# The opening of a sliding-window attention and feed-forward kernel: mask by a prefix sum, unshifted V for the first chunks, and another order of loads, scores and transposes

## The chip, the cores and the metric

One core of a Trainium2 chip (trn2) runs the whole program. The metric is device time in microseconds; the kernel before was run three times and its median is 326.21 us. A trace of one execution shows what each engine did: PE is TensorE, PEld its weight loads, DVE is VectorE, ACT is ScalarE, POOL is GpSimd, SP is SyncE. In the timeline rows the columns are start and duration in us, then engine, line, operation, output<-inputs, and in brackets the idle time before the row with what ended it.

## The reference

Attention with a causal window of 64 positions over 8 batches, 8 heads, 576 positions and 64 dimensions per head, and a gated feed-forward block (SiLU) on its output. Inputs and output are float32.

```python
def _attn_ref(q, k, v):
    scores = np.matmul(q, k.transpose(0, 1, 3, 2)) / np.sqrt(D)
    rel = pos[:, None] - pos[None, :]
    mask = (rel >= 0) & (rel < 64)
    scores = np.where(mask, scores, -1000000000.0)
    ...  # softmax over the last axis
    return np.matmul(attn, v)

def _moe_ref(x, w_gate, w_val, w_out):      # x: (4608, 512)
    g = x @ w_gate                          # (512, 1536)
    return (g * (1.0 / (1.0 + np.exp(-g))) * (x @ w_val)) @ w_out
```

## The kernel before

The 8 x 576 = 4608 tokens are cut into 36 chunks of 128. A chunk n holds two blocks of 64 queries. Each block sees its own 64 keys and the 64 before them, so the scores of a chunk are two triangles for each block: the lower one on its own keys, the upper one on the previous keys. One tile of 128 key rows by 128 query columns per head (`pt`) holds both.

Every operation is put on one engine's list, in the order in which the program names it (`_Graph.op`), and semaphores are added where data passes between engines. Each engine works through its list strictly in that order. The loads of q, k, v and of the weights are issued from POOL (`load`, `load2`, `load_w`); only the very first k load is issued from SP and ACT. Each POOL issue has a semaphore lane of its own, 16 in turn.

The program has an opening whose order is written by hand (`loads` and the first part of `build`), and a long remainder whose order stands in the lists `EARLY`, `LOADS` and `SHIPS`. The remainder chooses PSUM banks with a planner; the opening takes them from the list given to `banks`.

The opening goes like this:

- `warm(count, n)` issues matmuls on a tile of zeros (`wz`) into a PSUM bank that nobody reads: fillers.
- `first_loads` and `first_cast` bring the first 256 tokens of k, half by SP and VectorE, half by ACT and ScalarE. `first_T` transposes them on TensorE, `first_ev` copies them out.
- `load2` brings the first 256 tokens of q (stage 0) and the next 256 of k and q (stage 1); `T2` transposes them (L426) and copies them out.
- `init_ident` makes the identity with an affine select on POOL. `init_mask` makes three variants of the 0/1 mask of a chunk: two affine selects on POOL, then three instructions on VectorE (L333 to L335). `init_nmask` turns them into 0 and -30000.
- `Sa(n, True)` writes that bias into two PSUM banks with two 512-wide identity matmuls (L459); `Sb` adds the scores of chunk n (L479, L483) and lets ScalarE take the exponential (L491). From chunk 4 on the scores get no bias, and the 0/1 mask is multiplied in afterwards (`Sm`).
- The product of `pt` with V comes in three forms. `AVs` (L612) multiplies over all 128 key rows at once; as the rows of the first query block are not in the order of V's rows, it needs a copy of V shifted by 64 rows (`vs`, made by `shift` on POOL or ScalarE out of `va`). `AVmm` (L580) uses 64 x 64 quadrants of the array and reads `va` of this and the previous chunk directly; it has two phases of 16 matmuls, and phase 1 has a semaphore wait for phase 0. Chunk 0 has no predecessor and uses one matmul per head (L609).
- `AVn` divides by the row sums on VectorE: a reciprocal (L628) and a multiplication (L631).
- `X` transposes a finished chunk (L743) into `xT`, and `Fs` does the feed-forward for some of the 12 columns of 128: a gate block and a value block of matmuls (L818), a tanh on ScalarE (L825), and two VectorE instructions (L827, L829). The output multiplication is L850.

The PSUM data of phase 0 and phase 1 are joined in the array's accumulation; the wait between them is this argument of the second call:

```python
done.append(self.g.op("pe", pe, reads=rd, writes=[b[1] for b in bx],
                      after=done[0] if phase else None))
```

The functions that the change touches, and what calls them, with the line numbers of the profile before:

Of the kernel before, what the change touches and what calls it, by code (L numbers as in the profile page):

```python
# [7 lines left out]
ALU = mybir.AluOpType  # L8
# [158 lines left out]
class _Kernel:  # L167
# [41 lines left out]
    def alloc(self):  # L209
# [93 lines left out]
    def init(self):  # L303
        g = self.g
        self.zero(self.wup[:, :], ["wup"])
        g.op("act", lambda e: e.activation(self.wup[:, :], self.wup[:, :], ACTF.Exp), writes=["wup"])
        self.zero(self.wz[:, :], ["wz"])
        self.zero(self.ident[:, :], ["ident"])
        self.zero(self.mask[:, :], ["mask"], 1.0)
        self.init_va(0, 4)  # L310
        for i in range(3):
            self.zero(self.vs[i][:, :, 64:80], [("vs", i, 0), ("vs", i, 1)], 1.0)
# [9 lines left out]
            pattern=[[-1, 128]], channel_multiplier=1), writes=["ident"])  # L322

    def init_mask(self):
        g = self.g
        mm = self.mask[:, :].rearrange("p (v e q) -> p v e q", v=3, e=2)
        a, b = mm[:, :, 0, :], mm[:, :, 1, :]
        for fill, base in ((0.0, 0), (1.0, 64)):
            g.op("pool", lambda e, fill=fill, base=base: e.affine_select(
                out=a, in_=a, compare_op=ALU.is_ge, fill=fill, base=base,  # L330
                pattern=[[0, 3], [1, 64]], channel_multiplier=-1), writes=["mask"])
        src = mm[:, 0:1, 0, :].to_broadcast([128, 3, 64])
        one = g.op("dve", lambda e: e.tensor_scalar(b, src, -1.0, 1.0, ALU.mult, ALU.add), reads=["mask"], writes=["mask"])  # L333
        g.op("dve", lambda e: e.memset(mm[64:128, 1, 0, :], 0.0), writes=["mask"])
        g.op("dve", lambda e: e.memset(mm[0:64, 2, 1, :], 0.0), writes=["mask"], after=one)  # L335

    def init_nmask(self):
        self.g.op("dve", lambda e: e.tensor_scalar(
            self.nmask[:, :], self.mask[:, :], 1.0, 30000.0, ALU.subtract, ALU.mult), reads=["mask"], writes=["nmask"])

    def init_kmask(self):
        g = self.g
# [558 lines left out]
    def loads(self):  # L901
        self.first_loads()
        self.load2(0, "q")
        self.load2(1, "k")
        self.init()
        self.init_ident()
        self.first_cast("k", 0, "dve")
        self.init_mask()
        self.load2(1, "q")
        self.load(0, "v")  # L910
        self.load(1, "v")
        self.load(2, "v")
        self.load(3, "v")
        self.load_w("g", 0, 2)
        self.load_w("v", 0, 2)
# [81 lines left out]
    def main(self, t):  # L997
# [109 lines left out]
    def build(self):  # L1107
        F, S, AV, X, T2, O = self.F, self.S, self.AV, self.X, self.T2, self.O
        self.loads()
        self.banks("a", [0, 1, 2, 3, 4, 5, 6, 7, 0, 1, 4, 5, 2, 3, 0, 1, 6, 7, 4, 5, 2, 3, 0, 1, 6, 7, 2, 3])  # L1110
        self.banks("f", [4, 5, 0, 1, 6, 7, 2, 3])
        self.warm(84, n=58)
        self.first_cast("k", 1, "act")
        self.init_nmask()
        k0 = self.first_T("k")
        self.first_ev("k", k0, 0, "dve")
        self.first_ev("k", k0, 1, "act")
# [26 lines left out]
        self.AVs(a2)  # L1144
        self.AVn(a2)
        a3 = self.AVa(3)
        self.AVs(a3)
# [12 lines left out]
        next(f2, None)  # L1160
        next(f1)
        next(f1, None)
        for n in range(4):
# [54 lines left out]
```

## Time and profile before

| | |
|---|---|
| median of 3 runs | 326.21 us (326.02 to 330.19) |
| profiled execution, its own time | 325.66 us |
| its span, first to last instruction | 323.9 us |
| TensorE busy | 315.4 us, 97% |
| VectorE / ScalarE / POOL busy | 204.1 / 136.1 / 109.8 us |
| granted TensorE clock, mean | 1.000 |

The span lies within the execution's time; what is around it is start and end of the program. A share of busy time is a mean over stages, so the opening has to be read from its own rows. The chain of waits follows the work that ended last back to what released it.

### The profile page before, as it was taken

The numbers are of one execution on the slowest core, as the hardware profiler recorded it, in microseconds if no ns is written. First come the engines' busy times: TensorE is split into PE (matmuls) and PEld (weight loads), VectorE is DVE, ScalarE is ACT, GpSimd is POOL, SyncE is SP. The second block draws the span as 40 slices with busy tenths as digits, with TensorE's granted clock in tenths as the row PEclk, the third lists the DMA queues.
The fourth block names the chain that finished last, engine by engine and source line by source line (L and its number), as shares of the span: only waits on it lengthen the run. The fifth ranks groups of instructions, "written<-read, shape, count | busy, mean of one in ns | idle before, by whom it ended". The sixth has DMA issues, their size and how long they took to land.

```text
span 323.9 us, 7964 instructions
## 1 busy us (share of the span) xinstructions
PE 315.4 (97%) x3395; PEld 170.3 (53%) x3430; DVE 204.1 (63%) x355; ACT 136.1 (42%) x244; POOL 109.8 (34%) x138
## 2 busy tenths in 40 slices
PE   8899999999999999999999999999999999999996
PEld 7585588855455444545454444545454544444443
DVE  5678888853657738666657575756666566555510
ACT  4735854545354335433334343525252522322322
POOL 8999990007930703315050607070502000000000
DMA  9999999999999996969699989999976202000012
GB/s 145 176 190 169 170 175 153 143 140 120 141 156 143 117 161 111 151 163 150 147 159 166 157 137 113 134 127 135 119 119 74 67 34 64 35 32 33 32 67 97
DMA packets 165412, 39.85 MB, mean 123 GB/s; under 512 B 152705, under 2 KB 160641, under 8 KB 165377
## 3 DMA queue, kind: packets, MB, share of 16 engines
q0 software_dynamic: 115152, 18.62, 82.1%
q1 hardware_dynamic: 44896, 11.22, 26.0%
q10 hardware_dynamic: 5328, 9.51, 8.1%
q8 instruction: 27, 0.44, 0.6%
q14 instruction: 9, 0.07, 0.1%
HBM read 37.75 MB, written 9.44 MB: 146 GB/s over the span
## 4 chain that ended last, share of the span: by engine, by line
PE 92%; ACT 2%; DMA 2%; issue 1%; POOL 1%; DVE 0%; POOLq 0%
PE ps L818 57%; PE ps L850 28%; PE ps L661 2%; DMA va<-in_v_dram 2%; ACT pt L491 1%; PE ps L883 1%; PE ps L516 1%; ACT pt L528 1%; PE ps L479 1%; PE ps L423 1%; PE ps L743 1%; POOL qs L381 0%; PE ps L483 0%; PE ps L612 0%; ACT vs L296 0%
## 5 line engine op out<-in xcount | busy, mean ns | idle before, releaser
L818 PE MATMUL ps<-xT,Wv 128*128 128x512 bf16 (+1 forms) x486 | 110.5, 351 | 0.5
L818 PE MATMUL ps<-xT,Wg 128*128 128x512 bf16 (+1 forms) x479 | 107.6, 351 | 2.4 <-issue 1.4
L827 DVE SCALAR_TENSOR_TENSOR uu<-sig,ps 128x512 bf16<-128x512 bf16 (+1 forms) x109 | 74.0, 679 | 56.4 <-ACT sig L825 55.7
L825 ACT ACTIVATE sig<-ps 128x512 bf16<-128x512 f32 (+1 forms) x109 | 64.9, 597 | 79.8 <-PE ps L818 78.7
L850 PE MATMUL ps<-Wo,hT 128*128 128x512 bf16 x413 | 94.7, 379 | 0.6 <-ACT pt L491 0.3
L829 DVE SCALAR_TENSOR_TENSOR hT<-uu,ps 128x512 bf16<-128x512 bf16 (+1 forms) x109 | 74.3, 682 | 3.7
L818 PEld LDWEIGHTS ps<-xT,Wv 128*128 128x128 bf16 x496 | 48.5, 98 | 44.9
L369 POOL DMA_DIRECT2D kn<-in_k_dram x31 | 29.3, 949 | 122.8 <-PE ps L850 93.5
L818 PEld LDWEIGHTS ps<-xT,Wg 128*128 128x128 bf16 x496 | 46.6, 98 | 41.4
L850 PEld LDWEIGHTS ps<-Wo,hT 128*128 128x128 bf16 x420 | 40.9, 98 | 48.7
L857 ACT ACTIVATE ost<-ps 128x512 f32<-128x512 f32 x35 | 20.9, 597 | 89.9 <-PE ps L850 83.9
L369 POOL DMA_DIRECT2D va<-in_v_dram x40 | 36.0, 955 | 12.3 <-PE ps L850 12.3
L369 POOL DMA_DIRECT2D qn<-in_q_dram x31 | 29.5, 960 | 0.0
L688 DVE RECIPROCAL rp<-ps 128x14 f32<-128x14 f32 (+1 forms) x28 | 5.7, 203 | 36.0 <-PE ps L661 36.0
L491 ACT ACTIVATE pt<-ps 128x512 bf16<-128x512 f32 x36 | 19.0, 597 | 4.4 <-PE ps L483 4.1
L690 DVE TENSOR_TENSOR xb<-ps,rp 128x896 bf16<-128x896 f32 (+1 forms) x28 | 19.4, 692 | 1.0
L528 ACT ACTIVATE pt<-ps 128x512 bf16<-128x512 f32 x36 | 18.6, 602 | 2.3 <-PE ps L520 2.1
L661 PEld LDWEIGHTS ps<-va,pt 64*64 64x64 bf16 x888 | 10.8, 107 | 6.1 <-issue 5.5
L661 PE MATMUL ps<-va,pt 64*64 64x65 bf16 x888 | 13.4, 194 | 0.1
L543 DVE TENSOR_TENSOR pt<-pt,kmask 128x1024 bf16<-128x1024 bf16 x18 | 12.3, 684 | 0.0
L543 DVE TENSOR_TENSOR pt<-pt,mask 128x1024 bf16<-128x1024 bf16 x13 | 8.7, 686 | 0.8 <-ACT pt L491 0.8
L893 DVE COPY ost<-ps 128x128 f32<-128x128 f32 x1 | 0.3, 291 | 11.8 <-PE ps L883 11.8
(72 smaller groups left out, 151.0 us busy)
## 6 DMA issues: line engine op xcount, KB each, us to landing
out_dram<-ost ACTq DMA_DIRECT2D x35, 256.0 KB, 2.1
va<-in_v_dram POOLq DMA_DIRECT2D x32, 128.0 KB, 6.2
kn<-in_k_dram POOLq DMA_DIRECT2D x25, 128.0 KB, 4.9
qn<-in_q_dram POOLq DMA_DIRECT2D x25, 128.0 KB, 5.4
Wg<-in_moe_w_gate_dram POOLq DMA_DIRECT2D x6, 256.0 KB, 7.4
Wv<-in_moe_w_val_dram POOLq DMA_DIRECT2D x6, 256.0 KB, 7.1
Wo<-in_moe_w_out_dram POOLq DMA_DIRECT2D x2, 768.0 KB, 18.2
qs<-in_q_dram POOLq DMA_DIRECT2D x3, 256.0 KB, 8.6
```

The source lines that it names most:

```text
L369: self.g.op("pool", lambda e, d=d, a=a: e.dma_start(d, a), writes=ks, dma=True, after=self.hold)
L491: g.op("act", lambda e, po=po, p=p: e.activation(po, sv[p], ACTF.Exp, scale=SCALE), reads=[bx[p][1]], writes=[pk[p]])
L528: g.op("act", lambda e, po=po, p=p: e.activation(po, sv[p], ACTF.Exp, scale=SCALE), reads=[bx[p][1]], writes=[pk[p]])
L543: self.g.op("dve", lambda e: e.tensor_tensor(pt, pt, m, ALU.mult), reads=pk + [key], writes=pk)
L661: z = e.matmul(self.psa[64 * c:64 * c + 64, o:o + 65], pt[p][rows, h, 64 * a:64 * a + 64], va[m][rows, h, 0:65], start=first, stop=phase = ...
L690: g.op("dve", lambda e, d=d, num=num, rb=rb: e.tensor_tensor(d, num, rb, ALU.mult), reads=bk + [("rp", k)], writes=xk, cost=(1.0, 0.25)[k])
L818: r = e.matmul(bank[:, a * n:a * n + n], W[:, kk, f * 128:f * 128 + 128], xT[:, kk, lo:hi], start=(kk == 0), stop=(kk == NK - 1))
L825: g.op("act", lambda e, G=bank: e.activation(sig[:, 0:w], G[:, 0:w], ACTF.Tanh, scale=0.5), reads=[bk], writes=[("sig", i)])
L827: g.op("dve", lambda e: e.scalar_tensor_tensor(uu[:, 0:w], sig[:, 0:w], 1.0, G[:, 0:w], ALU.add, ALU.mult), reads=[("sig", i), gk], writes ...
L829: g.op("dve", lambda e: e.scalar_tensor_tensor(out, v3(uu), 0.5, v3(V), ALU.mult, ALU.mult), reads=[("uu", i), vk], writes=[("hT", ih, f) ...
L850: r = e.matmul(OB[:, :], hT[:, f, 128 * u:128 * u + 128], self.Wo[:, f, :], start=(f == 0), stop=(f == NF - 1), skip_group_check=mid is no ...
L857: g.op("act", lambda e: e.activation(ost[:, :], OB[:, :], ACTF.Copy), reads=[ok], writes=[("ost", io)])
```

## The change

It concerns the opening alone.

- The mask is made on VectorE: the identity is extended by its own first 64 columns, and `tensor_tensor_scan` runs along the columns adding the identity and subtracting the identity moved by 64 columns, starting from 0 for the first 64 rows and from 1 for the others (`edge`). The two affine selects on POOL go. `nmask` is made out of this one variant, in two variants in place of three. The other two variants of the 0/1 mask are copied in a new function, `init_masks`, which runs at the step `V` of the remainder.
- On POOL the identity comes ahead of the second k load; the second q load, the four V loads and the weights follow without anything between them.
- Chunks 1 to 3 use `AVmm` in place of `AVs`, so their six shifted copies (four on POOL, two on ScalarE) go.
- 40 fillers of 121 columns stand in place of 84 of 58; three fillers ahead of the second k transpose go, two come ahead of the second q transpose.
- The bias of chunk 2 comes ahead of product 0. The transposes of chunks 2 and 3 stand between the gate block and the value block of the first feed-forward step, and the second half of tokens for columns 0 and 1 comes ahead of the columns 2 and 3.

```diff
-        self.ident = sb("ident", 128)
+        self.id3 = sb("ident", 192)
+        self.ident = self.id3[:, 0:128]
+        self.edge = sb("edge", 1, F32)
...
-        self.nmask = sb("nmask", 3 * 128)
+        self.nmask = sb("nmask", 2 * 128)
...
-        self.zero(self.mask[:, :], ["mask"], 1.0)
+        self.zero(self.edge[0:64, :], [("edge", 0)])
+        self.zero(self.edge[64:128, :], [("edge", 1)], 1.0)
...
     def init_mask(self):
+        g.op("dve", lambda e: e.tensor_copy(self.id3[:, 128:192], self.id3[:, 0:64]), reads=["ident"], writes=["id3"])
+        g.op("dve", lambda e: e.tensor_tensor_scan(
+            self.mask[:, 0:128], self.id3[:, 0:128], self.id3[:, 64:192], self.edge[:, 0:1], ALU.add, ALU.subtract),
+            reads=["ident", "id3", ("edge", 0), ("edge", 1)], writes=["mask"])
+
+    def init_masks(self):
+        two = self.mask[:, 0:128].unsqueeze(1).to_broadcast([128, 2, 128])
+        out = self.mask[:, 128:384].rearrange("p (v x) -> p v x", v=2)
+        one = self.g.op("dve", lambda e: e.tensor_copy(out, two), reads=["mask"], writes=["mask"])
...  # two memsets of a quarter each, as before
-        for fill, base in ((0.0, 0), (1.0, 64)):
-            g.op("pool", lambda e, fill=fill, base=base: e.affine_select(
...
     def loads(self):
         self.first_loads()
         self.load2(0, "q")
-        self.load2(1, "k")
         self.init()
         self.init_ident()
+        self.load2(1, "k")
+        self.load2(1, "q")
+        self.init_mask()
+        self.init_nmask()
         self.first_cast("k", 0, "dve")
-        self.init_mask()
-        self.load2(1, "q")
-        self.load(0, "v")
...
-        self.load_w("g", 2, 4)
-        self.shift(0, 1, "pool")
-        self.shift(1, 1, "pool")
-        self.load_w("v", 2, 4)
-        self.shift(2, 1, "pool")
-        self.shift(3, 0, "pool")
-        self.W(4, 6)
-        self.W(6, 8)
+        for n in range(4):
+            self.load(n, "v")
+        for f in range(0, 8, 2):
+            self.W(f, f + 2)
...
         elif w == "V":
             self.init_va(4, self.NV)
+            self.init_masks()
...
-        self.warm(84, n=58)
+        self.warm(40, n=121)
...
         self.Sb(s0)
-        self.warm(3, j=0)
         T2(1, "k", ("dve", "dve"))
         self.Sb(s1)
+        self.warm(2, j=4)
         T2(1, "q", ("dve", "act"))
         self.start()
+        s2 = self.Sa(2, True)
         a0 = self.AVa(0)
         self.AVs(a0)
-        self.shift(1, 0, "act")
         self.AVn(a0)
-        s2 = self.Sa(2, True)
         self.Sb(s2)
-        self.shift(2, 0, "act")
         a1 = self.AVa(1)
-        self.AVs(a1)
+        self.AVmm(a1, 0)
+        self.AVmm(a1, 1)
...  # chunks 2 and 3 in the same way
         f0 = self.Fs(0, (0, 1), 0, 256)
         next(f0)
-        next(f0)
         X(2, "act", "a")
         X(3, "dve", "a")
+        next(f0)
         next(f0, None)
-        f1 = self.Fs(0, (2, 3), 0, 256)
-        next(f1)
         f2 = self.Fs(0, (0, 1), 256, 512)
         next(f2)
         next(f2)
         next(f2, None)
+        f1 = self.Fs(0, (2, 3), 0, 256)
+        next(f1)
         next(f1)
         next(f1, None)
```

More of the change, by code (lines that the diff above doesn't have):

```diff
@@ L325, in init_mask @@
         g = self.g
-        mm = self.mask[:, :].rearrange("p (v e q) -> p v e q", v=3, e=2)
-        a, b = mm[:, :, 0, :], mm[:, :, 1, :]
-        for fill, base in ((0.0, 0), (1.0, 64)):
[L329 to L335, printed above, removed]
+        g.op("dve", lambda e: e.tensor_copy(self.id3[:, 128:192], self.id3[:, 0:64]), reads=["ident"], writes=["id3"])
[3 more added lines that the diff above has]
+    def init_masks(self):
+        mm = self.mask[:, :].rearrange("p (v e q) -> p v e q", v=3, e=2)
+        two = self.mask[:, 0:128].unsqueeze(1).to_broadcast([128, 2, 128])
+        out = self.mask[:, 128:384].rearrange("p (v x) -> p v x", v=2)
+        one = self.g.op("dve", lambda e: e.tensor_copy(out, two), reads=["mask"], writes=["mask"])
+        one = self.g.op("dve", lambda e: e.memset(mm[64:128, 1, 0, :], 0.0), writes=["mask"], after=one)
+        self.g.op("dve", lambda e: e.memset(mm[0:64, 2, 1, :], 0.0), writes=["mask"], after=one)
     def init_nmask(self):
-        self.g.op("dve", lambda e: e.tensor_scalar(
-            self.nmask[:, :], self.mask[:, :], 1.0, 30000.0, ALU.subtract, ALU.mult), reads=["mask"], writes=["nmask"])
+        two = self.mask[:, 0:128].unsqueeze(1).to_broadcast([128, 2, 128])
+        out = self.nmask[:, :].rearrange("p (v x) -> p v x", v=2)
+        one = self.g.op("dve", lambda e: e.tensor_scalar(out, two, 1.0, 30000.0, ALU.subtract, ALU.mult), reads=["mask"], writes=["nmask"])
+        self.g.op("dve", lambda e: e.memset(self.nmask[64:128, 128:192], -30000.0), writes=["nmask"], after=one)
     def init_kmask(self):
@@ L1143, in build @@
         a2 = self.AVa(2)
-        self.AVs(a2)
+        self.AVmm(a2, 0)
+        self.AVmm(a2, 1)
         self.AVn(a2)
         a3 = self.AVa(3)
-        self.AVs(a3)
+        self.AVmm(a3, 0)
+        self.AVmm(a3, 1)
         self.AVn(a3)
```

8 lines of the change are left out of this document (1 added, 7 removed).

## The prediction

> **What bounds the kernel now.** I read the page first, then busy time by stretch, the chain of waits over the first 18 us, the transfers of that stretch, and last the timeline row by row. The page and the stretches:
>
> ```profile
> span 323.9 us, 7964 instructions
> PE 315.4 (97%) x3395; PEld 170.3 (53%) x3430; DVE 204.1 (63%) x355; ACT 136.1 (42%) x244; POOL 109.8 (34%) x138
> 0.00:16.00 16.00, 13.52 (x306) 10.11 (x308) 9.40 (x29) 9.14 (x16) 13.94 (x24) 1.00 1.44 160
> 66.00:314.00 248.00, 244.92 (x2431) 118.79 (x2458) 152.27 (x251) 97.27 (x174) 63.09 (x75) 1.00 1.04 113
> ```
>
> TensorE is the bound, and past the opening it hardly pauses (244.92 of 248 us busy). After the opening every engine's order of work is the same in both kernels but for three small mask instructions on VectorE. So the result is a shift of the point at which TensorE goes over to the dense feed-forward matmuls (L818, at 15.92 us). The ceiling of any gain is what TensorE does not do in the first 16 us: 16.00 - 13.52 = 2.5 us, under 0.8% of the time, and 1.3 of it lie before its first instruction.
>
> What leads to that point is told by the chain of waits:
>
> ```profile
> 6.27 6.03 DMA va<-in_v_dram
> ...
> 12.32 0.63 ACT vs L296
> ...
> 14.44 1.06 ACT pt L491 x2
> ...
> 15.54 0.44 PE ps L612 x14
> ```
>
> The second V chunk lands at 12.30 (6.27 + 6.03), ScalarE makes its shifted copy, TensorE multiplies with it, and so on to the last attention product (L612 at 15.54). The timeline has the same chain, with what stands around it:
>
> ```profile
> 1.29 4.24 PE L789 MATMUL ps<-wz 128*128 128x58 bf16 x84 [1.29 <-DVE wz L301]
> 2.33 0.88 POOL L381 DMA_DIRECT2D ks<-in_k_dram  x1
> 3.29 0.32 POOL L320 TENSOR_SCALAR_AFFINE_SELECT ident<-ident 128x128 bf16<-128x128 bf16 x1
> 3.54 0.87 POOL L329 TENSOR_SCALAR_AFFINE_SELECT mask<-mask 128x192 bf16<-128x192 bf16 x2
> 4.09 0.60 DVE L298 CAST ost<-hT 128x512 bf16<-128x512 f32 x1 [1.39 <-DMA hT<-in_k_dram]
> 4.50 0.91 POOL L381 DMA_DIRECT2D qs<-in_q_dram  x1
> 4.69 0.63 ACT L296 ACTIVATE ost<-hT 128x512 bf16<-128x512 f32 x1 [1.69 <-DMA hT<-in_k_dram]
> 5.12 0.34 DVE L338 TENSOR_SCALAR nmask<-mask 128x384 bf16<-128x384 bf16 x1
> 5.38 0.78 PE L769 MATMUL ps<-ident,ost 128*128 128x128 bf16 x8
> 5.99 0.59 PE L459 MATMUL ps<-nmask,ident 128*128 128x512 bf16 x2
> 8.62 0.82 PE L789 MATMUL ps<-wz 128*128 128x512 bf16 x3
> 8.74 1.08 ACT L491 ACTIVATE pt<-ps 128x512 bf16<-128x512 f32 x2 [0.95 <-PE ps L483]
> 10.64 0.64 PE L426 MATMUL ps<-ident,qs 128*64 128x128 bf16 x16 [0.27 <-DMA qs<-in_q_dram]
> 11.39 0.60 ACT L296 ACTIVATE qT<-ps 128x512 bf16<-128x512 bf16 x1
> 11.59 0.40 PE L609 MATMUL ps<-va,pt 128*128 128x65 bf16 x8 [0.31 <-DMA va<-in_v_dram]
> 13.01 0.22 PE L612 MATMUL ps<-vs,pt 128*64 128x65 bf16 x1 [0.20 <-ACT vs L296]
> 13.38 0.60 PE L459 MATMUL ps<-nmask,ident 128*128 128x512 bf16 x2
> 13.92 0.24 PE L479 MATMUL ps<-qT,kT 64*64 64x128 bf16 x2
> 14.29 0.62 PE L743 MATMUL ps<-ident,xb 128*128 128x128 bf16 x8
> 14.40 1.08 ACT L491 ACTIVATE pt<-ps 128x512 bf16<-128x512 f32 x2
> 15.92 0.28 PE L818 MATMUL ps<-xT,Wg 128*128 128x256 bf16 x1
> ```
>
> Read from it: product 1 starts at 13.01; the bias matmuls of scores 3 follow at 13.38 (0.37 later), the scores at 13.92 (0.54), the next matmuls at 14.29 (0.37); the two exponentials end at 15.48, 1.56 after the scores began; product 3 starts 0.06 later, the feed-forward 0.38 after that.
>
> **The change, part by part.**
>
> *Mask.* The two affine selects (0.87 us) leave POOL; VectorE gets a 64-column copy, a scan over 128 columns, an nmask of 256 columns and a memset. No row shows a scan. Its bounds are nothing and 0.69, twice the 384-column nmask of L338; I take 0.34, the row of L338 itself, the nearest. The identity now goes ahead of the k transfer on POOL and is ready near 2.33 + 0.08 + 0.32 = 2.73, so VectorE runs to about 3.8 and is free for its cast at 4.09. Cover: the first transposes wait for ScalarE's cast (4.69 + 0.63 = 5.32), so VectorE may be 0.6 us late. TensorE reads nmask first at 5.99, when it has long been ready (5.12 + 0.34 = 5.46): an earlier mask brings nothing by itself. Cost 0, with the worst scan too.
>
> *Fillers.* 84 x 58 = 4872 columns against 40 x 121 = 4840: the same 4.2 us, and the transposes start with the cast in either case. Of the three 512-wide fillers at 8.62, two come back later, ahead of the second q transpose, which waits for its transfer anyway. Cost 0.
>
> *Loads.* The second k load is issued about 0.45 us later (2.33 to 2.8), the second q load some 0.85 earlier, the four V loads 0.9 earlier, the later weights up to 4 us earlier, as the shifted copies that stood between them are gone. That helps only if the transfers waited for their issue:
>
> ```profile
> GB/s 0 0 0 0 70 139 340 393 221 166 173 159 163 178 153 155 196 146 150 157 155 155 154 156 169 178 194 195 197 196 197 224 183 190 193 191 197 194 197 198
> ```
>
> These are 40 slices of 0.5 us. From 2.5 us on there is no hole: the transfers run at a level rate with work queued, and they keep their order. So q still lands at 10.6 and V at 11.5 and 12.3. I take 0; the bound is the 0.85 us by which the issue moves.
>
> *No shifted V for chunks 1 to 3.* Each product goes from 16 matmuls over 128 rows (L612) to two phases of 16 quadrant matmuls (L580), where phase 2 waits for phase 1. No row has this pair back to back with 16; the last attention pair has it with 32, and a phase of 16 stands elsewhere:
>
> ```profile
> 269.34 1.00 PE L661 MATMUL ps<-va,pt 64*64 64x65 bf16 x64
> 270.50 0.81 PE L818 MATMUL ps<-xT,Wg 128*128 128x512 bf16 x3 [0.16 <-issue]
> 269.33 0.36 PEld L661 LDWEIGHTS ps<-va,pt 64*64 64x64 bf16 x32 [0.42 <-issue]
> 269.87 0.36 PEld L661 LDWEIGHTS ps<-va,pt 64*64 64x64 bf16 x32 [0.17 <-PE ps L661]
> 33.90 0.32 PE L580 MATMUL ps<-va,pt 64*64 64x65 bf16 x16
> 34.38 0.81 PE L818 MATMUL ps<-xT,Wg 128*128 128x512 bf16 x3 [0.16 <-issue]
> ```
>
> With 32 each, the second phase starts 0.54 after the first and the whole takes 1.00, so a phase lasts 0.46 and the hand-over 0.08. With 16 a phase lasts 0.32: the pair takes 0.32 + 0.08 + 0.32 = 0.72, and 0.16 pass before a full-width matmul (both rows of L818): 0.88 until the next work, against 0.37 to 0.38 for L612 now. Bounds: 0.48, if one phase vanished beside the other (33.90 to 34.38), and 1.16, that of the 32 form (269.34 to 270.50). I take 0.88, as it is built from 16-matmul rows.
>
> [...]
>
> *The chain, added up.* Product 1 now waits for V itself: 12.30 + 0.06 = 12.36 in place of 13.01, that is -0.65. Scores 2 must be done by then: q lands at 10.6, its ScalarE copy ends at 11.99 at the latest, the scores start at 12.0 and take 0.37, so it just fits. Product 1 costs +0.51 (0.88 - 0.37); bias and scores 3 to the end of their exponentials stay at 0.54 + 1.56; product 2 lies under those exponentials; product 3 costs +0.50 (0.88 - 0.38). The feed-forward starts at 12.36 + 0.88 + 0.54 + 1.56 + 0.06 + 0.88 = 16.28, against 15.92: **+0.36 us**.
>
> *Transposes 2 and 3 between gate and value.* Now they stand behind two blocks, afterwards behind one:
>
> ```profile
> 16.47 0.69 DVE L631 TENSOR_TENSOR xb<-ps,rc 128x512 bf16<-128x512 f32 x1
> 17.67 0.61 PE L743 MATMUL ps<-ident,xb 128*128 128x128 bf16 x8
> 18.15 1.92 PE L818 MATMUL ps<-xT,Wg 128*128 128x256 bf16 x16
> 28.55 0.69 DVE L827 SCALAR_TENSOR_TENSOR uu<-sig,ps 128x512 bf16<-128x512 bf16 x1 [0.32 <-ACT sig L825]
> ```
>
> The cover shrinks by one block, (17.67 - 15.92) / 2 = 0.87 us. Now the last scaling ends at 17.16, 1.62 after product 3 began (15.54). Afterwards product 3 begins at 15.40 and is 0.28 longer (0.72 - 0.44): the scaling ends at 17.30. The gate block ends at 16.28 + 0.87 = 17.15, chunk 2's transposes take 0.24, chunk 3's start at 17.39. It fits by hundredths: 0, and up to 0.4 if VectorE is later. The half-blocks that change places put the later-loaded weight columns last, so no new wait there.
>
> *Mask, second part.* A copy and two memsets join VectorE's work near 25 us, by the row of L338 at most 3 x 0.34 = 1.0, likelier 0.5. VectorE waits 0.32 us for ScalarE by 28.55, slack that takes most of it up; uncovered it would cost 0.5. I take 0.
>
> **The sum.** The profiled execution took 325.66 us: its span of 323.9 and 1.76 around it. 325.66 + 0.36 = 326.0. The median of the runs shown, 326.21, is 0.55 above that execution, so against the median 326.5 to 326.6; I say 326.5, +0.1%.
>
> **The rivals.**
>
> *A. The loads do come earlier, or the phases are cheap.* For: q and V are issued some 0.85 sooner. Against: the level rate above. If q lands at 9.8, its copy still waits on ScalarE for the exponentials of scores 0 and 1 (8.74 + 2 x 1.08 = 10.9), ends at 11.5, scores 2 start near 11.6 and product 1 near 11.97: -0.39, and the sum is 0.0, or 326.2. If instead the pair takes 0.48, it is 0.36 - 0.80 = -0.44, or 325.8; both together -0.83, or 325.4.
>
> *B. TensorE idles behind the transposes.* Chunk 3's transposes stand behind one block in place of two. At 0.4 us late the time is 326.9. For: it fits by hundredths. Against: VectorE has nothing else queued then.
>
> *C. The clock is lost.* With half as many matmuls in the warm-up and none at 8.62, the granted clock falls to half for part of the opening and stays there into the feed-forward, where every us of dense work then costs one more. At 7 us of it: 333.5. It gets out of 2% from 6.5 us of dense work at half rate on. Against: right behind the old fillers two 512-wide matmuls took 0.59 us (L459 at 5.99), full rate; the new fillers have the same columns; and the longest new pause is about 0.7 us, before 10.64. [...] The granted clock is 1.00 in the stretches shown.
>
> *D. The change does nothing that counts*, as V's landing sets the pace on both sides: 326.2, inside A.
>
> **How the numbers follow.** Forecast (V lands as before, pair near 0.88) 0.54; A with D 0.28; B 0.15; C 0.03. Range: low 325.3 is A's 325.4 less a tenth for the spread of the runs; high 327.2 is the sum with both pairs at 1.16 (326.5 + 2 x 0.28 = 327.1) and a tenth. It holds B, and leaves out C and some tails, under 2 in 10. About 2% (6.5 us) is what a measurement of this kernel can tell from no change: faster by that is beyond the 2.5 us ceiling, 0.01; slower 0.03, which is C; within 0.96.
>
> **What would show it.** Right: product 1 begins within 0.1 of V's landing, near 12.36; the bias about 0.88 later; a pause of about 0.1 between the phases; L818's first matmul between 16.1 and 16.5; no select of the mask on POOL. Wrong: the second V chunk landing before 12.0; a wait on VectorE ahead of chunk 3's transposes; a pair of 512-wide matmuls at much over 0.59 us after 6 us; or a wait behind 24 us that was not there.

## The result, and the profile after

The changed kernel took 329.24 us (median of 22 executions, 326.99 to 330.34) against 326.19 us of the kernel before (22 executions on the same chip). The ratio is 1.0078, 95% interval 1.0056 to 1.0099: **slower by 0.8%**, clear of no change by its interval, though under the 2% that the prediction took for the least that a measurement can tell. (Ratios, here and below, leave out executions more than 1.5% above the fastest of the same kernel.) The prediction of 326.5 us, range 325.3 to 327.2, was wrong, by 2.7 us. The profiled execution took 328.88 us, 3.22 more than the one profiled before.

The page of the kernel after (span and engines' busy time, then the granted clock in 40 slices, then the queue that carries instructions):

```profile
span 327.1 us, 7960 instructions
PE 316.9 (97%) x3397; PEld 171.2 (52%) x3433; DVE 205.2 (63%) x359; ACT 135.2 (41%) x242; POOL 106.7 (33%) x132
PEclk9989999999999999999999999999999999999999
q8 instruction: 27, 0.44, 0.6%
```

TensorE is busy 1.5 us longer than before with about as many instructions, and one slice of the opening has a lower clock. The timeline has the rest (start, duration, engine, line, operation, in brackets the idle time before the row; L4xx to L8xx of before are 8 lines further down here):

```profile
2.92 0.48 DVE L331 TENSOR_TENSOR_SCAN mask<-ident,edge 128x128 bf16<-128x128 bf16 x1
4.67 0.84 DVE L300 CAST ost<-hT 128x512 bf16<-128x512 f32 x1 [0.82 <-DMA hT<-in_k_dram]
5.66 0.61 PE L777 MATMUL ps<-ident,ost 128*128 128x128 bf16 x8 [0.33 <-DVE ost L300]
10.20 0.64 PE L434 MATMUL ps<-ident,qs 128*64 128x128 bf16 x16
11.80 0.19 PE L588 MATMUL ps<-va,pt 64*64 64x65 bf16 x1
12.47 0.60 PE L467 MATMUL ps<-nmask,ident 128*128 128x512 bf16 x2
13.00 0.24 PE L487 MATMUL ps<-qT,kT 64*64 64x128 bf16 x2
14.77 0.22 PE L491 MATMUL ps<-qT,kT 64*64 64x64 bf16 x2 [1.47 <-issue]
15.08 0.87 PE L751 MATMUL ps<-ident,xb 128*128 128x128 bf16 x8
15.88 1.67 PE L588 MATMUL ps<-va,pt 64*64 64x65 bf16 x64
17.48 1.62 PE L826 MATMUL ps<-xT,Wg 128*128 128x256 bf16 x8
18.94 0.61 PE L751 MATMUL ps<-ident,xb 128*128 128x128 bf16 x8
31.76 0.62 PE L431 MATMUL ps<-ident,qs 128*128 128x128 bf16 x8 [0.47 <-ACT kT L298]
```

Product 1 begins at 11.80, 1.2 us ahead of before, and scores 3 at 13.00, 0.9 ahead. Then, **in the middle of scores 3, TensorE stands still for 1.47 us** and waits for nothing that the profile shows ("issue"): q, k and the banks were there, since the same scores had begun. The matmuls behind it run slower: transposes 0.87 in place of 0.62, a gate block 1.62 in place of 1.05. The busy time by stretch has the reason, the granted clock (last column but two):

```profile
12.00:14.00 2.00, 1.21 (x40) 0.50 (x29) 1.49 (x3) 1.08 (x2) 2.00 (x4) 1.00 1.47 198
14.00:16.00 2.00, 1.23 (x32) 0.99 (x35) 0.44 (x2) 0.82 (x2) 2.00 (x4) 0.82 1.45 196
16.00:18.00 2.00, 1.85 (x67) 1.38 (x68) 1.47 (x5) 0.27 (x1) 2.00 (x4) 0.50 1.46 197
18.00:20.00 2.00, 2.00 (x21) 1.67 (x20) 1.06 (x2) 0.63 (x2) 2.00 (x5) 0.83 1.45 198
```

So the clock was halved for about 3.4 us (0.18 + 0.50 + 0.17 of 2 us each, lost, is 1.7 us of full clock) right behind the pause. Of the 22 executions 15 have a mean granted clock of 0.990 to 0.995 and a median of 329.39 us; the seven at 0.999 to 1.000 have 327.60. So most executions lose the clock as the traced one does, and those that keep it are still 1.4 us slower than before. Last, at 31.3 us there is a wait of 0.47 us for ScalarE that was not there before.

**The sum of the profiled execution.** By the prediction's chain from scores 3 on (1.56 + 0.06 + 0.88), the feed-forward would have begun at 13.00 + 2.50 = 15.50, 0.42 ahead of before. Pause +1.47; half clock in transposes and products +0.51 (0.87 - 0.62 and 1.67 against 1.41 for the same 64 at full clock in the last experiment): 17.48, as measured. Half clock in the first gate block +0.57. From there I compare the starts of the 109 tanh instructions of ScalarE in both traces, pair by pair: the kernel after is 2.10 us late at 22.7 us, 2.74 late from 30.5 on, 3.02 at 109 and 3.12 at the end. The step of 0.64 is the wait at 31.3; the last 0.4, between 95 us and the end, was not followed up.

### What the pause waits for

In the list of transfers the queue q8, "instruction", carries 27 packets of 16 KB in the whole run. Counted in the trace, TensorE had executed 447 instructions when it stopped (441 weight loads and matmuls, and 6 semaphore or drain instructions; all counts below are of this kind). It has 6,830 weight loads and matmuls on the page and 89 semaphore and drain instructions in the trace, 6,919 in all: one packet for 256 of them. One such packet ran at 12.45 to 13.41 us, 1.36 us before TensorE went on. That gave **theory 1**: TensorE gets its instructions in blocks of 256; the next block is asked for when the one before it begins, and runs on the DMA engines beside the loads (q8 in the page above, 0.6% of their time); where 256 instructions are executed sooner than the next block is there, TensorE stops. When a block is asked for is not seen in a trace; that it is when the one before it begins fits the table below. The rivals: the quadrant products are dear by themselves (theory 2), or the clock is lost for another reason (theory 3). The packets of 16 KB, one for 256 instructions, and the boundaries below, 256 apart (447 and 703 executed), agree with theory 1. What a fetch costs is told by the table.

All from the traces, in us ("begins" is the first instruction of the block, "reached" the start of the last instruction ahead of the next block, "goes on" the first one in it):

| kernel | block begins | packet of the next block | boundary reached | goes on |
|---|---|---|---|---|
| before, at 447 executed | 6.21 | 8.21 to 9.28 | 12.55 | 12.55, no pause |
| before, at 703 | 12.55 | 15.82 to 16.72 | 19.8 | 19.91, no pause |
| **after, at 447** | 8.91 | 12.45 to 13.41 | 13.09 | **14.77** |
| after with 84 fillers, at 447 | 6.10 | 9.56 to 10.50 | 11.55 | 12.10 |
| the same, at 703 | 12.10 | 15.88 to 16.82 | 15.45 | 18.14 |
| before with quadrant products, at 703 | 12.76 | 16.33 to 17.31 | 16.13 | 18.59 |
| before with cut fillers, at 703 | 11.27 | 16.06 to 17.01 | 16.73 | 18.43 |
| after with shifted V, at 447 | 8.66 | 12.06 to 13.00 | 12.96 | 14.40 |
| after, later transfers held, at 447 | 9.23 | 10.29 to 11.18 | 13.41 | 13.41, no pause |

In these rows, wherever there was a pause, TensorE went on 1.3 to 1.6 us after the packet had landed, and 5.7 to 6.1 us after the block before had begun (7.2 with cut fillers). The latter is no fixed time: in the four rows at 703 the packet ran between 15.82 and 16.33 us, though the block before had begun anywhere from 11.27 to 12.76. In the kernel before, 256 instructions take 6.3 and 7.3 us at these two places. In the kernel after, the block that begins at 8.91 holds two long fillers and no long wait, and else transposes, scores with their bias, product 0 and the 64 instructions of a quadrant product: 4.2 us.

### The profile page after: what moved, and what is told of

Its sections match the earlier page's. It is cut to its first block, busy times and chain, and to the rows that moved or that the text cites. A ratio compares the mean times of both kernels' runs of the same rounds, so it can differ in the third digit from the quotient of the medians.

```text
span 327.1 us, 7960 instructions
## 1 busy us (share of the span) xinstructions
PE 316.9 (97%) x3397; PEld 171.2 (52%) x3433; DVE 205.2 (63%) x359; ACT 135.2 (41%) x242; POOL 106.7 (33%) x132
## 4 chain that ended last, share of the span: by engine, by line
PE 95%; issue 2%; ACT 1%; DMA 1%; DVE 0%
PE ps L826 57%; PE ps L858 28%; PE ps L669 2%; DMA hT<-in_k_dram 1%; PE ps L487 1%; PE ps L588 1%; PE ps L524 1%; PE ps L891 1%; PE ps L751 1%; PE ps L491 1%; PE ps L467 1%; ACT pt L499 1%; ACT pt L536 1%; PE ps L434 1%; PE ps L431 1%
## 5 line engine op out<-in xcount | busy, mean ns | idle before, releaser
L491 PE MATMUL ps<-qT,kT 64*64 64x64 bf16 x280 | 7.6, 194 | 1.5 <-issue 1.5
## 6 DMA issues: line engine op xcount, KB each, us to landing
Wo<-in_moe_w_out_dram POOLq DMA_DIRECT2D x2, 768.0 KB, 22.7
```

## The experiments

Each was timed against the kernel before on the same chip; the ratio stands with its 95% interval.

### 84 fillers in the changed kernel

```diff
-        self.warm(40, n=121)
+        self.warm(84, n=58)
```

> The changed kernel with the old fillers (84 of 58 columns), that is 88 more TensorE instructions (a matmul and its weight load each) ahead of everything else, in the same time. Theory (instruction fetch): TensorE stops in scores 3 at 13.30 us because the next 16 KB of its instructions have not arrived; it had then executed 447 instructions. With 88 more ahead, the same count is reached near the start of product 1 (about 11.9 us), and the fetch is asked for earlier, near 7 us, when less is queued: no pause in scores 3. The next block ends 256 instructions on (703), at the first feed-forward block near 15.5 us, and a pause of 1 to 2 us may come up there. Time 326.0 to 328.5. Rival (the pause belongs to scores 3 behind a quadrant product, whatever the count): pause of about 1.5 us at the same place, 329 us.

332.18 us (330.49 to 335.84), ratio 1.0162 (1.0116 to 1.0208). The timeline:

```profile
12.10 0.22 PE L491 MATMUL ps<-qT,kT 64*64 64x64 bf16 x2 [0.35 <-issue]
18.14 0.23 PE L588 MATMUL ps<-va,pt 64*64 64x65 bf16 x5 [2.50 <-issue]
```

Scores 3 run through; a short pause stands at 447 executed instructions, and a longer one at 703, in product 3. With 88 instructions more in the warm-up the same boundaries fall into earlier work, as theory 1 has it; the pause went along with the count of instructions and not with the place in the program. The time lies over the 326.0 to 328.5 us expected: the longer pause is 2.50 us, and the clock stood at 0.50 from 19.1 to 22.6 us. The old number of fillers thus doesn't save the changed kernel.

### 40 fillers in the kernel before

```diff
-        self.warm(84, n=58)
+        self.warm(40, n=121)
```

> The kernel before with the new fillers alone (40 of 121 columns): 88 TensorE instructions fewer, nothing else. Theory (instruction fetch): the fetch packet that ran at 8.2 us now runs near 12.5, and TensorE stops after about 447 instructions, which here is at the transposes of chunks 0 and 1 or product 2, about 14.5 us; the pause is 0.2 to 1 us, of which 0.3 lie under an old wait for the exponentials. 326.2 to 327.2, and to 329 in executions in which the pause costs the clock. Rival (the fillers are harmless, the loss comes from quadrant products and order): 326.2, no new pause.

329.82 us (327.82 to 335.56), ratio 1.0086 (1.0048 to 1.0124). The fillers alone, with the same columns, cost as much as the whole change. Where:

```profile
5.35 1.04 PE L769 MATMUL ps<-ident,ost 128*128 128x128 bf16 x8
35.32 0.82 PE L818 MATMUL ps<-xT,Wg 128*128 128x512 bf16 x3 [0.85 <-issue]
106.55 0.81 PE L818 MATMUL ps<-xT,Wg 128*128 128x512 bf16 x3 [2.28 <-ACT pt L491]
```

The pause expected near 14.5 us did not come (the block before began at 10.04, the packet ran at 12.01, and the boundary was crossed at 14.29), but all later boundaries have moved by 88 instructions, and two of them, at 957 and at 2999 executed (as recorded; some matmul records are missing), now come right behind dense attention work. The last row names ScalarE's exponentials, but in the trace of before the same matmul starts 0.63 us into them; the packet ran until 105.0, and TensorE went on 1.5 us later. The transposes at 5.35 took 1.03 to 1.06 us here, in two other traces with 40 fillers and in one with 84, 0.93 in two more with 84, and 0.61 to 0.81 in the other eight, of both forms; the number of fillers doesn't separate them.

### Later transfers held

```diff
-        for n in range(4):
+        for n in range(2):
             self.load(n, "v")
-        for f in range(0, 8, 2):
-            self.W(f, f + 2)
...  # V2, V3 and all weights issued on POOL once TensorE has done scores 1
```

> The changed kernel, but POOL issues V of chunks 2 and 3 and all weights only when TensorE has done scores 1 (about 9.6 us). TensorE's instructions are the same. Theory (instruction fetch behind queued transfers): the fetch asked for near 9 us finds less ahead of it, its packet runs before 11.5 in place of 12.45, and the pause in scores 3 shrinks to under 0.4 us; the granted clock stays at 1.0; 325.8 to 327.0. Rival (the pause has to do with the instruction mix alone): pause of 1.5 us as before, 329 us or more, as the weights are later too.

331.78 us (331.3 to 333.33), ratio 1.0159 (1.0126 to 1.0193). The timeline, and the stretch after the block was asked for (GB/s last):

```profile
16.89 0.94 PE L588 MATMUL ps<-va,pt 64*64 64x65 bf16 x32 [1.91 <-DMA va<-in_v_dram]
10.00:12.00 2.00, 1.84 (x45) 1.20 (x43) 1.50 (x4) 1.80 (x4) 1.64 (x2) 1.00 0.42 33
```

The loads issued by then (V0 and V1, landed at 10.19 and 11.02) were running out, 157 GB/s from 9.5 to 10.0 us and 33 over the stretch above, and the packet ran there, 1.06 us after its block began, in place of 3.54; the boundary at 13.41 was crossed without a pause. So the fetch waits behind the loads. What was won there was lost again, as V and then the weights came late (waits of 1.91 and 1.15 us) and the clock stood at 0.50 for 6.8 us.

### 10 long fillers

```diff
-        self.warm(40, n=121)
+        self.warm(10, n=484)
```

> The changed kernel with 10 fillers of 484 columns: the same columns, 60 TensorE instructions fewer than the changed kernel has. Theory (instruction fetch at fixed counts): TensorE stops 60 instructions further along in its work, in product 2 or the transposes ahead of it (about 14.0 us), for 1 to 2 us, and scores 3 run through. 327 to 329.5. Rival (the pause belongs to scores 3): at 13.3 us as in the changed kernel.

329.28 us (327.73 to 331.0), ratio 1.0091 (1.0058 to 1.0123).

```profile
15.60 1.24 PE L588 MATMUL ps<-va,pt 64*64 64x65 bf16 x58 [1.46 <-issue]
```

60 instructions fewer, and the pause, as long as before, stands in product 2, again at 448 executed.

### Shifted V back in the changed kernel

```diff
-        self.AVmm(a1, 0)
-        self.AVmm(a1, 1)
+        self.AVs(a1)
...  # so for chunks 2 and 3, and the six copies at their old places
```

> The changed kernel with the shifted copies of V and the 16-matmul product back for chunks 1 to 3; the 40 fillers, the mask and the new order stay. Theory 1 (TensorE gets its instructions in blocks of 256, and in this stage the next block is usable only some 6.0 us after the block before it began: 8.91 to 14.77 us in the changed kernel, 12.10 to 18.14 with 84 fillers in it): the block still begins near 8.9, product 1 has 32 instructions fewer, so the block boundary moves 32 instructions on, to the end of scores 3 near 13.7, and a pause of about 1.0 us stays there with no visible releaser; 328 to 329.5 us. Theory 2 (the quadrant products are the loss): three pairs by 0.3 to 0.5 us go, no pause is left, 326 to 327 us.

328.46 us (326.55 to 330.91), ratio 1.0061 (1.0035 to 1.0087).

```profile
14.40 0.62 PE L751 MATMUL ps<-ident,xb 128*128 128x128 bf16 x8 [1.25 <-issue]
15.65 1.05 PE L826 MATMUL ps<-xT,Wg 128*128 128x256 bf16 x8
```

The boundary moved 32 instructions on, to the end of scores 3, and the pause stayed (1.25 us; 1.0 was expected). Theory 2, no pause, fails.

### Quadrant products alone

```diff
-        self.AVs(a1)
+        self.AVmm(a1, 0)
+        self.AVmm(a1, 1)
...  # so for chunks 2 and 3; the six copies go; kernel before
```

> The kernel before with the two-phase quadrant products for chunks 1 to 3 and without the six shifted copies; its 84 fillers, mask and order stay. Theory 1 (blocks of 256 instructions, 6.0 us each in this stage): the three products have 96 instructions more, so the block that began at 12.5 us runs out at about 15, in product 2 or 3, instead of 19.91 in the dense matmuls; the next one is usable near 18.5. TensorE stands still for 3 to 3.5 us there, the granted clock falls after it, and the time is 329.5 to 332 us. Theory 2 (the sum of the prediction, pair against single product): 326.2 + 0.4 = 326.6 us and no pause.

333.32 us (332.47 to 334.26), ratio 1.0218 (1.0197 to 1.0239). Timeline and stretches:

```profile
18.59 0.25 PE L580 MATMUL ps<-va,pt 64*64 64x65 bf16 x6 [2.28 <-issue]
51.01 0.43 PE L580 MATMUL ps<-va,pt 64*64 64x65 bf16 x14 [2.35 <-issue]
18.00:20.00 2.00, 1.41 (x18) 1.24 (x18) 0.90 (x2) 0.14 (x1) 2.00 (x4) 1.00 1.45 197
52.00:54.00 2.00, 2.00 (x11) 1.40 (x10) 1.08 (x3) 0.60 (x1) 0.00 (x0) 0.50 1.88 150
```

The pause stands where the count of instructions put it, at 704 executed. It is shorter than the 3 to 3.5 us expected, since TensorE came there only at 16.1. A second one of the same kind, at 1468 executed, was not expected; only behind that one did the clock fall. Its packet ran from 46.53 to 48.83 us, longer than the others, and TensorE went on 2.2 us after it, so the 1.3 to 1.6 us of the table don't hold there. With the second pause the time lies over the 329.5 to 332 us expected. In the trace this kernel is 2.81 us late behind the first pause and 6.87 behind the second.

### The planner's costs mended

```diff
-        one = self.g.op("dve", lambda e: e.tensor_copy(out, two), reads=["mask"], writes=["mask"])
+        one = self.g.op("dve", lambda e: e.tensor_copy(out, two), reads=["mask"], writes=["mask"], cost=0.2)
...  # 0.05 for each of the two memsets of init_masks
```

> The changed kernel, its program the same but for the costs that the planner of PSUM banks is told for the three instructions of the second part of the mask: 0.2, 0.05 and 0.05 us in place of 0.61 each. Theory: the planner believed VectorE 1.5 us later than it is and so took a bank that ScalarE had just been given; the 0.47 us of TensorE idle at 31.3 us, ahead of the q transposes (released by ScalarE's copy to kT), go, and the time falls by 0.4 to 0.5 us, to 328.7. Rival: the wait has another cause, or another takes its place: 329.0 to 329.4 us.

327.71 us (326.6 to 330.57), ratio 1.0045 (1.0013 to 1.0077).

```profile
31.83 0.61 PE L431 MATMUL ps<-ident,ks 128*128 128x128 bf16 x8
32.27 0.61 PE L431 MATMUL ps<-ident,qs 128*128 128x128 bf16 x8
```

The wait between the two is gone; the step in the starts of the tanh there is 0.20 us in place of 0.64. So 0.44 us came from three VectorE instructions that the planner took for 0.61 us each. The two medians differ by more, 1.5 us, but the intervals of the two ratios overlap, and the trace is of the slowest of the twelve executions (330.57), so I claim only what the traces show.

### 84 fillers, one quadrant product

```diff
-        self.warm(40, n=121)
+        self.warm(84, n=58)
...
-        self.AVmm(a2, 0)
-        self.AVmm(a2, 1)
+        self.AVs(a2)
...  # so for chunk 3, with their copies; costs mended
```

> The changed kernel with 84 fillers of 58 columns, quadrant product for chunk 1 alone, shifted V and 16-matmul products for chunks 2 and 3, and the planner's costs mended. Theory 1 (blocks of 256 instructions, some 6.0 us each in this stage): blocks begin near 6.1 and 12.1 us; the first boundary stays at 11.55 with a pause of 0.5, the second moves 64 instructions on, from 15.45 in product 3 into the dense matmuls near 18.9, where the next block is there; so no long pause and no half clock. The feed-forward starts near 15.4 in place of 15.92 and the time is 325.2 to 326.0 us, at or under the kernel before. If a pause over 1 us stays, or the time is over 327, theory 1 is wrong or not the whole.

327.85 us (325.8 to 332.49), ratio 1.0019 (0.9976 to 1.0063).

```profile
15.46 1.05 PE L826 MATMUL ps<-xT,Wg 128*128 128x256 bf16 x8
```

No long pause in the trace (an execution of 325.95 us), clock full, the feed-forward 0.46 us ahead of before, as expected. The median was not: it lies over 327, and by the test set beforehand theory 1 is then wrong or not the whole. The trace has what theory 1 says; seven of the twelve executions lie above 326.5 us, no trace of one of these was taken, and what delays them is not shown. By the trace the lead shrinks to 0.13 at 22.7 us (0.18 of it in a short stop at the boundary at 18.25) and turns to 0.18 late at the end.

### Five fillers of before cut into 40

```diff
-        self.warm(2, j=0)
+        self.warm(16, n=64, j=0)
...
-        self.warm(3, j=0)
+        self.warm(24, n=64, j=0)
```

> The kernel before with its five 512-wide fillers between the first scores cut into 40 of 64 columns: the same columns on the same zeros, 70 more TensorE instructions (matmuls and weight loads), nothing else touched. Theory 1 (blocks of 256 instructions, each usable some 6.0 us after the one before it began, in this stage): the block that began at 12.55 us now begins near 12.2, and it runs out 70 instructions earlier, near 16 us at the start of the feed-forward, in place of 19.91; the next one is usable near 18.2, so TensorE stands still for about 2 us there with no visible releaser, and the time is 328 to 330 us. Rival (fillers cost what their columns cost, as the prediction took it): no pause, 326.2 us.

327.66 us (326.67 to 330.64), ratio 1.0021 (0.9987 to 1.0055).

```profile
8.31 0.63 PE L789 MATMUL ps<-wz 128*128 128x64 bf16 x16
9.22 0.87 PE L789 MATMUL ps<-wz 128*128 128x64 bf16 x24
18.43 0.38 PE L818 MATMUL ps<-xT,Wg 128*128 128x256 bf16 x2 [1.42 <-issue]
```

The cut fillers take what the long ones took (0.59 and 0.82 before). Nothing else differs but 70 instructions on zeros, and a pause appears in the first gate block, where the count had put it; the trace is 1.80 us late from there on, 1.96 at the end. The pause is shorter than the 2 us expected, and the time lies under 328. The clock stayed at 1.00, so the pause needs no loss of clock (theory 3). This is the plainest evidence for theory 1. The ratio doesn't resolve it, as the executions of the kernel before were spread widely in this comparison (median 326.94).

### All products shifted, 84 fillers

```diff
-        self.AVmm(a1, 0)
-        self.AVmm(a1, 1)
+        self.AVs(a1)
...  # chunks 2 and 3 too; five copies on POOL, one on VectorE; costs mended
         T2(0, "q", ("act", "dve"))
+        self.init_masks()
```

> The changed kernel (mask by the scan, its order of loads, scores and transposes) with 84 fillers of 58 columns and with shifted V and 16-matmul products for chunks 1 to 3: the copies for chunks 2 and 3 and half of that for chunk 1 on POOL behind four weight loads, the other half for chunk 1 on VectorE; the second part of the mask is made at 8 us, where VectorE waits, instead of at 25. Theory 1 (blocks of 256 instructions): as many TensorE instructions as the kernel before within 4, so the block boundary behind product 1 lies past 19 us and the next block is there; no pause over 0.3 us in the opening. The exponentials of scores 3 follow those of scores 2 without a copy between them, and the feed-forward begins near 15.1 us in place of 15.92: span 323.1 to 323.6, time 324.8 to 325.4 us where nothing later disturbs it. Rival: the gain of 0.8 us is lost to a wait for a copy on POOL or VectorE ahead of product 1 or 2: 325.5 to 326.3 us.

332.74 us (332.0 to 333.32), ratio 1.0154 (1.0102 to 1.0205): a miss of my own making.

```profile
14.78 0.23 DVE L339 COPY mask<-mask 128x256 bf16<-128x256 bf16 x1 [6.36 <-POOL vs L300]
16.54 1.04 PE L467 MATMUL ps<-nmask,ident 128*128 128x512 bf16 x2 [5.50 <-DVE kT L300]
```

The copies on POOL declare that they read the mask, the new writer of the mask stood behind them, and all of VectorE's list waited.

### The same with the mask ahead of the copies

```diff
         self.first_cast("k", 0, "dve")
+        self.init_masks()
...
         T2(0, "q", ("act", "dve"))
-        self.init_masks()
```

> The kernel of the run before this one with one instruction group moved: the second part of the mask is made right behind VectorE's first cast, ahead of the copies of V on POOL. In the run before it stood behind them in the program, the copies on POOL name the mask as read, and VectorE waited 6.36 us for them. With that wait gone theory 1 (blocks of 256 instructions) stands to the same test: no pause over 0.3 us in the opening, the feed-forward near 15.1 us in place of 15.92, span 323.1 to 323.6 and 324.8 to 325.4 us where nothing later disturbs it. Rival: the copies on POOL still end too late for product 1 or 2, or the second load of q lets nothing come earlier: 325.5 to 326.3 us.

326.53 us (325.33 to 332.41), ratio 1.0005 (0.9975 to 1.0035).

```profile
12.15 0.28 DVE L300 COPY vs<-va 64x512 bf16<-64x512 bf16 x1 [0.81 <-DMA va<-in_v_dram]
15.40 1.05 PE L826 MATMUL ps<-xT,Wg 128*128 128x256 bf16 x8
```

No pause over 0.3 us, but V lands at 12.13 again, so product 1 waits for VectorE's copy and the feed-forward begins at 15.40 and not near 15.1. The trace ends 0.10 us ahead of before. This is the best version found, and it can't be told from the kernel before.

### Weights held, costs mended

```diff
+        self.wh = [o for o in self.g.ops if o.eng == "pe"][-1]
...  # all eight weight loads on POOL behind scores 1; V as in the changed kernel
```

> The changed kernel with the planner's costs mended, and with all eight weight loads of the opening held on POOL until TensorE has done scores 1 (about 9.7 us), in place of 7.8 us on; 40 fillers, quadrant products and the four V loads stay. It asks what the block of instructions waits behind: the block that TensorE needs at 13.1 us is asked for near 8.9, and its packet ran at 12.45. Theory 1a (it waits behind the weights that POOL has issued by then): its packet runs near 11, the pause in scores 3 shrinks from 1.47 to under 0.5 us, and the time is 325.4 to 326.4 us. Theory 1b (it waits behind what was issued earlier, the V loads above all, whose last lands at 12.56): the packet still runs near 12.4, the pause stays at 1.3 to 1.6 us, and the time is 327 to 329 us, as with the costs mended alone. Rival to both: the weights come too late and the feed-forward waits for them: a wait on a weight load ahead of the first gate block.

327.83 us (327.46 to 330.0), ratio 1.006 (1.0042 to 1.0078).

```profile
14.23 0.22 PE L491 MATMUL ps<-qT,kT 64*64 64x64 bf16 x2 [0.92 <-issue]
15.09 1.41 PE L588 MATMUL ps<-va,pt 64*64 64x65 bf16 x64
21.44 0.38 PE L826 MATMUL ps<-xT,Wv 128*128 128x256 bf16 x2 [0.95 <-issue]
```

Between the two expectations: the packet ran at 11.89, 2.97 us after its block began, in place of 3.54 in the changed kernel and 3.48 with the costs mended alone, and the pause shrank to 0.92. So holding the weights takes some 0.5 us off the wait; with V2 and V3 held as well it was 1.06, so most of it is behind those two. The next packet took 4.75 us from its block's begin (3.83 in the changed kernel), and a second pause stands at 703 executed; that the held weights are the reason is my reading. The trace is of the slowest of six executions.

## Why the prediction was wrong, step by step

- **"So the result is a shift of the point at which TensorE goes over to the dense feed-forward matmuls"** failed twice. It counted work and waits and took instructions to be free; and it took the planner's remainder to be fixed. Two of the prediction's own signs of being wrong showed, V1 before 12.0 us and a new wait behind 24 us, but none of them looked for a lack of instructions.
- **Fillers, cost 0, "same columns".** This is the step that failed first. The columns were the same and the warm-up as long (1.23 + 4.10), but 84 fillers are 88 instructions more than 40. The block boundary that lay harmless in scores 2 at 12.55 now closed one of the program's dense stretches, 256 instructions in 4.2 us where the kernel before takes 6.3. On the kernel before, the fillers alone gave 1.0086. Yet with 84 fillers the changed kernel gave 1.0162: what failed is not the number 40 but that the sum has no term for the supply of instructions, which measured 1.47 us and the half clock behind it.
- **Quadrant products, +0.51 and +0.50.** Their time was over-estimated: product 1 to the bias is 12.47 - 11.80 = 0.67, not 0.88, within the bounds; the 0.16 on the way out did not show. Their true price is 32 more instructions each, which the sum did not have: alone they cost 1.0218 through two pauses.
- **The way in, cost 0.** The sum has 0.16 on the way out of a product and nothing on the way in. The row at 11.80 has no idle time ahead of it, but the scores ahead of it are 64x64 matmuls too, and so is product 2 ahead of product 3; only product 2 stands behind full-width work. Where that is at full clock, the row at 15.09 of the last experiment, behind full-width transposes (14.54 to 15.16), has no idle time ahead of it either. So nothing was due there.
- **Loads, cost 0.** Wrong in the other direction: V0 and V1 were complete at 10.00 and 10.85 (11.46 and 12.30 before), 1.45 us earlier against a bound of 0.85, and product 1 began at 11.80 and not at 12.36; rival A was right in this. Product 1 no longer waited for V: it came 0.95 us after V1, right behind scores 2, with TensorE busy up to it. In the landing records, the 16 parts of V1 are spread over 1.7 us in the kernel before, where an instruction packet ran at 8.21, and over 0.5 us in the kernel after, where it ran at 12.45. Of the fourteen traces ten split in this way (1.0 to 1.7 us where the packet ran ahead of V1, 0.4 to 0.7 where it ran later); three don't (1.35 in the kernel before with 40 fillers, 1.44 with the costs mended, 1.0 in the last experiment), and in one the packet ran as V1 landed. So that this is the cause was not shown.
- **Earlier loads as a cost.** Not in the sum at all: the first fetch took 3.0 to 3.7 us from the begin of its block to its packet in the versions with the new order of loads, 1.4 to 2.0 in the four with the old one, and 1.06 where only V0 and V1 had been issued. With 84 fillers the block begins at 6.10 in the new order and at 6.21 in the old one, and its packet runs at 9.56 and at 8.21. The edit that was to bring V earlier is thus a part of the pause.
- **Mask, cost 0.** Right: the scan took 0.48, within 0 to 0.69, and the bias matmuls did not wait. The 0.3 us at the first transposes has another reason: the later half of k landed as late as before (the cast starts at 4.67, against 4.69), but it was VectorE's this time, whose cast took 0.84 us where ScalarE's had taken 0.63.
- **Transposes 2 and 3, cost 0.** No wait shows at 18.94, but the pause had moved it. In the two versions without a pause they begin 0.88 and 0.89 behind the start of the gate block and last 0.81 and 0.93 in place of 0.61, so some 0.2 to 0.3 us of rival B was there.
- **Mask, second part, cost 0.** VectorE's time was free, as I said; its planned time was not (0.44 us). I had looked for the 0.5 ("uncovered it would cost 0.5") on the wrong path.
- **Rival C, the clock**, had the right loss at the wrong place: it came behind the pause, not behind the fillers, and lasted 3.4 us, not 7. The kernel before with 40 fillers, which has no pause in the opening, kept a clock of 1.00 there. In the traces it stood at 0.50 behind pauses of 1.47, 1.63, 2.35 and 2.50 us and stayed at 1.00 behind pauses of 1.25, 1.42, 1.46 and 2.28. So a pause of 1.47 us can be followed by a loss of clock. The length of the pause alone doesn't settle it, and what does is open.

What stays open: why a third to a half of the executions of the two versions without a long pause in their trace take 2 us or more longer than that trace, and the last 0.4 us of the profiled execution.

## What to carry to other kernels

Count instructions, not only columns and microseconds: where 256 consecutive TensorE instructions (weight loads, matmuls and semaphore instructions) take less than about 6 us (5.3 to 7.2 at the pauses of the opening) and loads run beside them (some 150 to 200 GB/s in this opening), TensorE may run dry, and adding or removing anything ahead of that place, fillers too, moves the boundary. An idle time marked "issue" in the middle of a group of matmuls, with a packet on the instruction queue landed 1.3 to 1.6 us before it ends, is how it looked in these profiles. And tell a planner the true cost of small instructions; three wrong ones cost 0.44 us.

## What the runs showed of the hardware

- The instruction queue carries 27 packets of 16 KB on the DMA engines, one for 256 of TensorE's 6,919 instructions; a packet takes 0.9 to 1.1 us itself in the opening, and where TensorE stood still for it, it went on 1.3 to 1.6 us after it had landed (2.2 once, at 51.01 us in the kernel before with quadrant products).
- The wait from the begin of a block to the packet of the next grew with what was queued: 1.06 us with two V loads running out, 2.0 in the kernel before, 3.0 with V but no weights, and 3.5 in the kernel after. It was 7.3 once (25.81 to 33.10 in the kernel before with 40 fillers), which was not followed up.
- The granted clock fell to 0.50 behind a pause of 1.47 us, and not behind one of 2.28 us. Where it fell, it stayed there for 3.4 us (this kernel, and three others) or 6.8 us (later transfers held, and the run with VectorE's wait of 6.36 us).
- 16 fillers of 64 columns took 0.63 us, two of 512 columns 0.59: cutting a filler costs next to no time, and 28 instructions.
